# Attention row maxima: the third maximum of a step as two 256-key matmuls, and the second score pair's exponentials one bank each

## Chip, cores and metric

The kernel runs on one NeuronCore of a Trainium2 chip. The metric is the device time of one execution in microseconds (us). Before the change it is 3601.7 us, the median of 3 runs (3599.2 to 3603.54).

## What is computed

Two layers of two sublayers each on x of shape 2048 x 512, in float32. The first sublayer mixes by a Fourier transform, written as matmuls with given matrices. The second is attention with 32 heads of width 16 that share one key and one value head:

```python
q = (x @ wq).reshape(B, S, H, Dh).transpose(0, 2, 1, 3)
k = x @ wk
v = x @ wv
scores = jnp.einsum("bhqd,bkd->bhqk", q, k) * (Dh ** -0.5)
p = softmax(scores, axis=-1)
o = jnp.einsum("bhqk,bkd->bhqd", p, v)
return o.transpose(0, 2, 1, 3).reshape(B, S, H * Dh) @ wo
```

Each sublayer is added to its input, which is layer-normalised first.

## The kernel before

Each layer has a phase A (Fourier mixing, layer norm, queries, keys, values) and a phase B (attention). The change lies in phase B and in the short preparation at the end of phase A. The order of the instructions is written out by hand in the code; nothing reorders them. The tile pools add the waits: a write into a tile waits until the tile's earlier readers are done, and a read until its writers are.

**Steps.** Phase B has 16 query tiles of 128 rows (`i`), and 32 steps for each (`s_`): two halves of the heads by 16 chunks of 128 keys. A step (`phase_b`, the loop at L1049) does four things.

- Four *scores* (`score`, L879): matmuls of 64 contraction rows by 512 columns (four pairs of heads by 128 queries). `j` is 0 to 3; `j % 2` is the half of the array's rows (0 to 63 or 64 to 127) that a matmul uses, since even and odd heads lie on different halves. Two matmuls on different halves can run side by side. Scores 0 and 1 go to the two banks of one PSUM tile `x`, scores 2 and 3 to those of another (`pair`, two buffers of two banks). When both scores of a pair are issued, one exponential of 1024 elements reads both banks (ScalarE, L899).
- Up to three *maxima* for a later query tile (`max_half`, L435, by way of `more_max`): a matmul of 64 rows by 512 keys for one head into a bank `y` (three buffers), then a maximum over its 512 elements on VectorE into the tile `mxp` (`reduce_max`, recorded at L102). The row maximum is subtracted inside the score matmul, through extra contraction rows, so the maxima of a tile must be ready before its scores start. `units` lists all (tile, pair, half, key block) in order, `owed` keeps three per step.
- The *value matmuls* (`pv`, L903) of the step two before: four matmuls of 128 rows by 512 into four column groups of one bank `z`. Each is two records in the trace.
- At given steps, pieces of the output projection of the tile before (`out_tasks`), stores and loads, and `max_neg`, `max_split` and `max_rows`, which turn `mxp` into the extra rows.

In TensorE's queue a step is: value matmuls, first score, one maximum, second score, two maxima, third score, fourth score. With `g` the half of the next maximum, the scores are issued so that matmuls on different halves alternate: `1-g`, max `g`, `g`, max `1-g`, max `g`, `1-g`, `g`.

In the last tile of a layer, once all maxima are done, scores 2 and 3 go to banks `y` of their own, with an exponential of 512 elements each (L889 and L891).

`mxp` holds for each pair and half the maxima of 4 key blocks (5 for tile 0). `max_neg` takes the maximum over them.

Of the kernel before, what the change touches and what calls it, by code (L numbers as in the profile page):

```python
# [17 lines left out]
P = 128  # L18
# [3 lines left out]
DH = 16  # L22
# [25 lines left out]
def fnet_mqa_kernel(ctx: ExitStack, tc: tile.TileContext, x_in, ct, dt_, wq, wkv, wo, out):  # L48
# [5 lines left out]

    def f(ap):
        return ap.bitcast(F32)

    class Pace:
        pe = dve = act = pool = at = 0.0
# [61 lines left out]
    def pair():  # L121
        return ps.tile([P, 2, 512], F32, name="x", bufs=2)
# [127 lines left out]
    def make_layer(L, src, mid, dst, last):  # L250
# [138 lines left out]

        def partial(i):  # L390
            if i not in o.mxp:
                o.mxp[i] = sb.tile([P, NPAIR, 2, 4 if i else 5], F32, name=f"mxp{i % 4}")
                for e, (i_, kb) in enumerate(KEPT):
                    if i == i_:
                        np_ = taken[i, kb]
                        if np_:
                            pool.tensor_copy(o.mxp[i][:, :np_, :, kb], st["mxe"][:, e, :np_])
            return o.mxp[i]
# [36 lines left out]
        def max_half(i, pr, g, kb):  # L435
            pm = bank("y")
            gs = slice(64 * g, 64 * g + KR)
            mm(pm, o.qT[i][gs, pr, :], kz[gs, kb * 512:kb * 512 + 512], start=True, stop=True)
            vec.reduce_max(partial(i)[:, pr, g, kb:kb + 1], pm, axis=AX.X)

        def qT_load(i, k=None):
            k_ = QSLOT[i] if k is None else k
            if k_ in ("h", "l"):
                qt = (xnh if k_ == "h" else xnl)[:, 12:, :].rearrange("p t n -> p (t n)")
            else:
                qt = slot(k_, F32R)
            nc.sync.dma_start(f(qt), qd[i])
            o.qT[i] = qt.rearrange("p (a q) -> p a q", a=NPAIR)
            if k is None:
                o.loaded.add(i)  # L450

        def max_neg(i, p0=0, n=NPAIR, k=4, whole=False):
            nm = sb.tile([P, NPAIR, 2], F32, name="nm")[:, :n, :]
            vec.tensor_reduce(nm, o.mxp[i][:, p0:p0 + n, :, :k], op=ALU.max, axis=AX.X, negate=True)
            if p0 + n == NPAIR:
                o.mxp.pop(i)
            st["nm"] = nm
            if whole:
                max_split()

        def max_split():
            nmv = st.pop("nm").rearrange("p a g -> p g a")
            n = nmv.shape[2]
            ms = sb.tile([P, 2, 2, NPAIR], F32, name="ms").rearrange("p g r a -> p (g r a)")
            ms = ms[:, :4 * n].rearrange("p (g r a) -> p g r a", g=2, r=2)
            vec.tensor_copy(ms[:, :, 0, :].bitcast(F32R), nmv)
            vec.tensor_sub(ms[:, :, 1, :].bitcast(F32R), nmv, ms[:, :, 0, :])
            st["ms"] = ms
# [170 lines left out]
        def phase_a(extra):  # L639
# [211 lines left out]
            for e, left in ahead.items():  # L851
                assert EARLY[e][0]
                taken[EARLY[e][:2]] = NPAIR - len(left)
            units.extend((0, pr, g, 3) for pr in range(HALF, NPAIR) for g in range(2))
            units.extend((i, pr, g, kb) for i in range(1, NT) for pr in range(NPAIR) for kb in range(4) for g in range(2)
                         if pr >= taken.get((i, kb), 0))
            max_neg(0, 0, HALF, 5, True)
            for k in range(12):
                more_max()
                if k == 2:  # L860
                    max_rows(0, 0, HALF, nc.scalar)

        units = []
        o.done = o.extra = 0

        def more_max():
            if o.done < len(units) and units[o.done][0] in o.loaded | {0}:
                max_half(*units[o.done])
                o.done += 1

        def owed(n):
            return min(3 * (n + 1) + 12 + o.extra, len(units)) - o.done

        def done_with(i, pr):
            return all(u[:2] > (i, pr) for u in units[o.done:])

        ptiles = {}

        def score(i, s_, j):  # L879
            hf, c = divmod(s_, NT)  # L880
            jj, g = divmod(j, 2)
            cp = 4 * (2 * hf + jj)
            if (i, s_) not in ptiles:
                k = i * NSTEP + s_
                ptiles[i, s_] = slot((6, 7, 2)[k % 3]).rearrange("p (j n) -> p j n", j=4)
            w = j // 2
            if i == NT - 1 and jj == 1 and o.done == len(units):
                e = bank("y")
                nc.tensor.matmul(e, kz[64 * g:64 * g + KR, c * P:(c + 1) * P],  # L889
                                 o.qT[i][64 * g:64 * g + KR, cp:cp + 4, :], start=True, stop=True)  # L890
                nc.scalar.activation(ptiles[i, s_][:, j, :], e, AF.Exp, scale=DH ** -0.5)  # L891
                return
            first = "e" not in st
            if first:
                st["e"] = pair()
            nc.tensor.matmul(st["e"][:, g, :], kz[64 * g:64 * g + KR, c * P:(c + 1) * P],  # L896
                             o.qT[i][64 * g:64 * g + KR, cp:cp + 4, :], start=True, stop=True)
            if not first:
                nc.scalar.activation(ptiles[i, s_][:, 2 * w:2 * w + 2, :], st.pop("e"), AF.Exp, scale=DH ** -0.5)  # L899

        acc = {}

# [62 lines left out]
        def o_proj(i):  # L965
            for k in range(NK):
                o_mm(k)
                if k == NK - 1:
                    o_add(i)
                if k % 2 and 3 <= i < NT - 1:  # L970
                    for _ in range(2):
                        more_max()
                        o.extra += 1

        def o_add(i):
            nc.vector.tensor_add(bt["x"], bt["po"], bt["x"])
# [61 lines left out]
        def phase_b(nxt):  # L1038
# [7 lines left out]
            for j in range(NK):  # L1046
                wo_load(j)
            behind = []
            for n in range(NT * NSTEP):  # L1049
                i, s_ = divmod(n, NSTEP)  # L1050
                if len(behind) == 2:
                    pv(*behind.pop(0))
                behind.append((i, s_))
                g = units[o.done][2] if o.done < len(units) else 1
                for j, m in ((1 - g, 1), (g, 2), (3 - g, 0), (2 + g, 1)):
                    score(i, s_, j)
                    for _ in range(m):
                        if owed(n) >= 1:
                            more_max()
                if i == 0 and 2 <= s_ <= 8 and s_ % 2 == 0:  # L1060
                    q_half_store(14, s_ // 2 - 1)
                if n == 12:
# [13 lines left out]
                for at, j, p0, np_ in ((NT - AHEAD, i, HALF, HALF), (NSTEP - AHEAD, i + 1, 0, HALF if i == NT - 2 else NPAIR)):  # L1076
                    if j in (0, NT - 1) or j == i + 1 < NT:
                        if s_ == at:
                            assert done_with(j, p0 + np_ - 1), (n, j, o.done, len(units), units[o.done], owed(n))
                            max_neg(j, p0, np_)  # L1080
                        if s_ == at + 1:
                            max_split()
                        if s_ == at + 2:
                            max_rows(j, p0, np_)
# [71 lines left out]
```

## Time and profile before

One execution was profiled. It took 3602.02 us as a whole, and its span in the profile is 3600.2 us.

| what | value |
|---|---|
| median of 3 runs | 3601.7 us |
| profiled execution: its time, its span | 3602.02 us, 3600.2 us |
| phase B of layer 0, from its first to its last value matmul | 644.2 to 1800.4 us |
| phase B of layer 1, the same | 2433.2 to 3588.2 us |
| granted TensorE clock over the span | 0.997 of full speed |

How to read the lines that the prediction shows: in a timeline row stand the start, the duration, the engine, the line of the code, the operation, the tile written and the tiles read, the shapes and how many were merged; in brackets the idle time of that engine before it and what ended it. PE is TensorE's matmuls, PEld its weight loads, DVE VectorE, ACT ScalarE, POOL GpSimd. Matmuls are pipelined, and the end of a matmul is modelled. In a table of stretches each engine has its busy time with the number of instructions; then follow the granted TensorE clock, the DMA share and GB/s.

### The profile page before, as it was taken

The numbers are of one execution on the slowest core, as the hardware profiler recorded it, in microseconds if no ns is written. First come the engines' busy times: TensorE is split into PE (matmuls) and PEld (weight loads), VectorE is DVE, ScalarE is ACT, GpSimd is POOL, SyncE is SP. The second block draws the span as 40 slices with busy tenths as digits, with TensorE's granted clock in tenths as the row PEclk, the third lists the DMA queues.
The fourth block names the chain that finished last, engine by engine and source line by source line (L and its number), as shares of the span: only waits on it lengthen the run. The fifth ranks groups of instructions, "written<-read, shape, count | busy, mean of one in ns | idle before, by whom it ended". The sixth has DMA issues, their size and how long they took to land.

```text
span 3600.2 us, 63751 instructions
## 1 busy us (share of the span) xinstructions
PE 3551.6 (99%) x25090; PEld 1901.3 (53%) x25090; DVE 2801.6 (78%) x4819; ACT 2390.8 (66%) x3050; POOL 781.9 (22%) x976
## 2 busy tenths in 40 slices
PE   8999999999999999999999999999999999999999
PEld 6787877434333433343377878773433343333433
DVE  6186987888888888888311979878888888888882
ACT  4323232888888888888933232229888888888888
POOL 5544342011211111111264343420000000000000
PEclk9999999999999999999999999999999999999999
DMA  5544242211111100110144343422111111011100
GB/s 181 140 140 134 99 137 60 75 49 37 34 32 51 34 23 22 49 34 25 40 141 113 128 118 106 130 60 86 34 35 34 50 35 34 22 29 43 35 24 25
DMA packets 204445, 240.85 MB, mean 67 GB/s; under 512 B 36848, under 2 KB 160752, under 8 KB 197232
## 3 DMA queue, kind: packets, MB, share of 16 engines
q1 hardware_dynamic: 199216, 219.98, 20.5%
q0 software_dynamic: 4864, 16.78, 1.6%
q8 instruction: 196, 3.21, 0.4%
q14 instruction: 105, 0.86, 0.1%
q10 hardware_dynamic: 64, 0.02, 0.0%
HBM read 172.48 MB, written 63.17 MB: 65 GB/s over the span
## 4 chain that ended last, share of the span: by engine, by line
PE 85%; DVE 7%; ACT 2%; issue 1%; DMA 1%; SPq 0%; POOL 0%; DVEq 0%; ACTq 0%; POOLq 0%
PE z L910 27%; PE y L78 19%; PE x L896 19%; PE x L78 17%; DVE mxp L102 4%; PE z L78 1%; DVE mxe L102 1%; ACT slot L899 1%; PE z L83 1%; ACT slot L891 0%; PE y L889 0%; DVE row L102 0%; DVE bst L102 0%; DVE ms L102 0%; PE y L83 0%
## 5 line engine op out<-in xcount | busy, mean ns | idle before, releaser
L102 DVE TENSOR_REDUCE mxp<-y 128x1 f32<-128x512 f32 (+1 forms) x3472 | 2166.7, 679 | 267.3 <-PE y L78 218.1
L899 ACT ACTIVATE slot<-x 128x1024 f32<-128x1024 f32 x1992 | 1943.4, 1027 | 313.6 <-PE x L896 226.4
L910 PE MATMUL z<-slot,v 128*32 128x512 f32 x8192 | 1096.4, 605 | 1.7 <-ACT row L913 1.7
L78 PE MATMUL y<-kz,slot 64*128 64x512 f32 (+1 forms) x3048 | 980.1, 424 | 4.4 <-DVE kz L102 2.1
L896 PE MATMUL x<-slot,kz 64*128 64x512 f32 x2960 | 891.2, 447 | 0.8 <-DMA slot<-mt 0.8
L896 PEld LDWEIGHTS x<-slot,kz 64*128 64x128 f32 x2960 | 368.1, 185 | 734.3 <-ACT slot L899 599.7
L78 PEld LDWEIGHTS y<-kz,slot 64*128 64x128 f32 x3048 | 487.8, 185 | 121.8 <-DVE mxp L102 26.5
L78 PE MATMUL x<-ch,xnh 64*128 64x512 f32 (+2 forms) x2048 | 531.6, 372 | 11.7 <-ACT xnh L102 9.5
L78 PE MATMUL x<-ch,xnl 64*128 64x512 f32 (+2 forms) x2048 | 527.8, 364 | 1.0 <-POOL xnl L102 0.6
L78 PE MATMUL x<-cl,xnh 64*128 64x512 f32 (+2 forms) x2048 | 524.3, 364 | 0.4 <-POOL cl L102 0.4
L950 POOL TENSOR_TENSOR row<-row,row 128x256 f32<-128x256 f32 x63 | 46.3, 734 | 1573.7 <-DMA row<-rd 1184.2
L102 POOL TENSOR_TENSOR cl<-craw,ch 128x512 fp32r<-128x512 f32 x244 | 318.0, 1321 | 298.2 <-ACT ch L102 243.0
L78 PEld LDWEIGHTS x<-ch,xnh 64*128 64x128 f32 (+1 forms) x2048 | 293.1, 185 | 63.4 <-issue 16.2
L78 PEld LDWEIGHTS x<-ch,xnl 64*128 64x128 f32 (+1 forms) x2048 | 298.7, 185 | 38.0 <-POOL xnl L102 4.4
L78 PEld LDWEIGHTS x<-cl,xnh 64*128 64x128 f32 (+1 forms) x2048 | 295.0, 185 | 32.2 <-POOL cl L102 0.7
L910 PEld LDWEIGHTS z<-slot,v 128*32 128x32 f32 x8192 | 163.7, 108 | 274.6 <-issue 247.5
L102 ACT COPY junk<-x 128x2 f32<-128x2 f32 x236 | 37.7, 160 | 350.6 <-PE x L78 328.0
L102 DVE TENSOR_REDUCE mxe<-y 128x1 f32<-128x512 f32 x408 | 257.1, 679 | 9.8 <-PE y L78 9.6
L102 ACT CAST ch<-craw 128x512 fp32r<-128x512 f32 x264 | 158.8, 620 | 155.7 <-PE x L78 120.2
L78 PE MATMUL y<-slot,slot 128*128 128x512 f32 x816 | 216.4, 406 | 8.2 <-DVE mxp L102 6.7
L78 PEld LDWEIGHTS y<-slot,slot 128*128 128x128 f32 x816 | 144.7, 188 | 63.1 <-issue 28.2
L896 PE MATMUL x<-xnl,kz 64*128 64x512 f32 x512 | 154.5, 443 | 0.3 <-DMA xnl<-mt 0.3
(126 smaller groups left out, 2576.9 us busy)
## 6 DMA issues: line engine op xcount, KB each, us to landing
craw<-ct_in SPq DMA_DIRECT2D x112, 512.0 KB
slot<-qd SPq DMA_DIRECT2D x42, 1024.0 KB
qd<-row SPq DMA_DIRECT2D x144, 128.0 KB
od<-row SPq DMA_DIRECT2D x252, 64.0 KB
row<-x_in SPq DMA_DIRECT2D x32, 256.0 KB
mid<-row POOLq DMA_DIRECT2D x32, 256.0 KB, 2.6
craw<-ct_in SPq DMA_DIRECT2D x32, 256.0 KB
row<-mid SPq DMA_DIRECT2D x32, 256.0 KB
```

What stands on the lines that cost most here:

```text
L78: nc.tensor.matmul(out_, w, x, **k)
L83: nc.tensor.transpose(out_, x, i_)
L102: return fn(out_, in_, *a, **k)
L896: nc.tensor.matmul(st["e"][:, g, :], kz[64 * g:64 * g + KR, c * P:(c + 1) * P], o.qT[i][64 * g:64 * g + KR, cp:cp + 4, :], start=True, sto ...
L899: nc.scalar.activation(ptiles[i, s_][:, 2 * w:2 * w + 2, :], st.pop("e"), AF.Exp, scale=DH ** -0.5)
L910: nc.tensor.matmul(a[32 * j:32 * j + 32, :], v1[:, c, :], pt[:, j, :], start=c == 0, stop=c == NT - 1)
L950: nc.gpsimd.tensor_mul(bt["ot"][:, cs], bt["ot"][:, cs], bt["den"][:, cs])
```

## The change

Per step, two of the maxima stay whole 512-key matmuls, one on each half of the rows, now issued together as a pair (`max_whole`). The third (`max_couple`) covers half of a key block, 256 keys, for both heads of a pair: one 256-key matmul on half 0 as the first of the step's 64-row matmuls, one on half 1 as the last, both into one bank, and one VectorE maximum over 2 x 256 elements. Two row halves write one bank, so an explicit dependency keeps them apart: `relay` puts a no-op on ScalarE that waits for the first 256-key matmul, and the second waits for the no-op. The second 256-key half of the block is taken up in the next step that owes a maximum, and gets a column of its own; so `mxp` has 6 columns, of which unused ones are filled by a GpSimd memset, and `max_neg` reads 6. `max_neg` and `max_split` use parts of the tiles `row0` or `row2` for their results.

The two `x` tiles of the scores are now allocated once per layer (`o.pairs`). Scores are issued in the order 1, 0, 3, 2. The first pair keeps its exponential of 1024 elements (`exp_pair`). In the second pair each score is followed by an exponential of 512 elements of its own.

```diff
+    def behind_(later, first):
+        tc.add_manual_dep(later.ins, first.ins.name,
+                          mybir.DependencyInfo(mybir.DependencyClass.Sync, mybir.DependencyReason.DATA), reason="row halves")
...
-                o.mxp[i] = sb.tile([P, NPAIR, 2, 4 if i else 5], F32, name=f"mxp{i % 4}")
+                o.mxp[i] = sb.tile([P, NPAIR, 2, 6], F32, name=f"mxp{i % 4}")
+                nc.gpsimd.memset(o.mxp[i][:, HALF if i == 0 else 0:, :, 4:6], -3.0e38)
...
+        def max_whole(i, pr, kb):
+            for g in range(2):
+                max_half(i, pr, g, kb)
+
+        def max_couple(i, pr, kb, h, g):
+            if g == 0:
+                st["couple"] = bank("y").rearrange("p (g c) -> p g c", g=2)
+            gs = slice(64 * g, 64 * g + KR)
+            c0 = 512 * kb + 256 * h
+            m = nc.tensor.matmul(st["couple"][:, g, :], o.qT[i][gs, pr, :], kz[gs, c0:c0 + 256], start=True, stop=True)
+            if g == 0:
+                st["first"] = m
+                return
+            behind_(m, st.pop("relay"))
+            k = kb
+            if h:
+                k = 4 + o.coupled.get((i, pr), 0)
+                o.coupled[i, pr] = k - 3
+                assert k < 6
+            nc.vector.reduce_max(partial(i)[:, pr, :, k], st.pop("couple"), axis=AX.X)
+
+        def relay():
+            st["relay"] = nc.scalar.nop()
+            behind_(st["relay"], st.pop("first"))
...
-        def max_neg(i, p0=0, n=NPAIR, k=4, whole=False):
-            nm = sb.tile([P, NPAIR, 2], F32, name="nm")[:, :n, :]
+        def max_neg(i, p0=0, n=NPAIR, k=6, whole=False):
+            st["gather"] = half(0 if i or p0 else 2)
+            nm = st["gather"][:, 64:64 + 2 * n].rearrange("p (a g) -> p a g", g=2)
...
-            first = "e" not in st
-            if first:
-                st["e"] = pair()
-            nc.tensor.matmul(st["e"][:, g, :], kz[64 * g:64 * g + KR, c * P:(c + 1) * P],
+            e = o.pairs[w]
+            nc.tensor.matmul(e[:, g, :], kz[64 * g:64 * g + KR, c * P:(c + 1) * P],
                              o.qT[i][64 * g:64 * g + KR, cp:cp + 4, :], start=True, stop=True)
-            if not first:
-                nc.scalar.activation(ptiles[i, s_][:, 2 * w:2 * w + 2, :], st.pop("e"), AF.Exp, scale=DH ** -0.5)
+            if w:
+                nc.scalar.activation(ptiles[i, s_][:, j, :], e[:, g, :], AF.Exp, scale=DH ** -0.5)
+
+        def exp_pair(i, s_):
+            nc.scalar.activation(ptiles[i, s_][:, :2, :], o.pairs[0], AF.Exp, scale=DH ** -0.5)
...
+            o.pairs = [pair(), pair()]
             for n in range(NT * NSTEP):
                 i, s_ = divmod(n, NSTEP)
                 if len(behind) == 2:
                     pv(*behind.pop(0))
                 behind.append((i, s_))
-                g = units[o.done][2] if o.done < len(units) else 1
-                for j, m in ((1 - g, 1), (g, 2), (3 - g, 0), (2 + g, 1)):
-                    score(i, s_, j)
-                    for _ in range(m):
-                        if owed(n) >= 1:
-                            more_max()
+                whole = pick_whole(n)
+                couple = pick_couple(n)
+                if couple:
+                    max_couple(*couple, 0)
+                score(i, s_, 1)
+                score(i, s_, 0)
+                if couple:
+                    relay()
+                exp_pair(i, s_)
+                if whole:
+                    max_whole(*whole)
+                score(i, s_, 3)
+                score(i, s_, 2)
+                if couple:
+                    max_couple(*couple, 1)
```

TensorE's queue over one step in the middle of phase B of layer 0, before the change. `x` are the scores, `y` the maximum's matmuls, `z` the value matmuls; a bracket names the engine whose semaphore the matmul waits for:

```order
L896 MATMUL x<-xnl,kz 128x512 [waits Activation_49]
L78 MATMUL y<-kz,slot_9473 128x512 [waits DVE_49]
L896 MATMUL x<-xnl,kz 128x512
L78 MATMUL y<-kz,slot_9473 128x512 [waits DVE_49] x2
L896 MATMUL x<-xnl,kz 128x512 [waits Activation_49]
L896 MATMUL x<-xnl,kz 128x512
L910 MATMUL z<-slot_11376,v_74 32x512 x4
```

The first score of each pair waits for ScalarE (Activation), the second does not. The same place after the change:

```order
L455 MATMUL y<-kz,slot_10386 128x256 [waits DVE_49]
L945 MATMUL x<-xnl,kz 128x512 x2
L82 MATMUL y<-kz,slot_10386 128x512 [waits DVE_49] x2
L945 MATMUL x<-xnl,kz 128x512 [waits Activation_49] x2
L455 MATMUL y<-kz,slot_10386 128x256 [waits Activation_sequencer_49]
L962 MATMUL z<-slot_11630,v_74 32x512 x4
```

The 256-key matmuls stand first and last; the scores of the first pair (1 and 0) carry no wait of their own, and both scores of the second pair (3 and 2) wait for ScalarE. ScalarE's queue over one step after the change:

```order
L951 ACTIVATE slot_12958<-x 128x1024 [waits PE_49,Activation_49]
L948 ACTIVATE slot_12958<-x 128x512 [waits PE_49] x2
```

Before, two exponentials of 1024 elements stood there. Now one of 1024 is followed by two of 512, score 3's and then score 2's, each waiting for its own matmul (PE); the no-op of `relay` stands ahead of them and is not shown.

## Prediction before the run

> **What bounds the kernel now.** I read the page first (busy shares, slices, chain), then the time of the two attention phases, then one step of them instruction by instruction. Four lines of the page:
>
> ```profile
> span 3600.2 us, 63751 instructions
> ...
> PE 3551.6 (99%) x25090; PEld 1901.3 (53%) x25090; DVE 2801.6 (78%) x4819; ACT 2390.8 (66%) x3050; POOL 781.9 (22%) x976
> ...
> PEclk9999999999999999999999999999999999999999
> ...
> PE 85%; DVE 7%; ACT 2%; issue 1%; DMA 1%; SPq 0%; POOL 0%; DVEq 0%; ACTq 0%; POOLq 0%
> ```
>
> TensorE is busy throughout and carries 85% of the chain that ended last. The change touches only the loop over 512 steps in each attention phase. Those phases are the stretches below (busy time of TensorE, its weight loads, VectorE, ScalarE, GpSimd, then the granted clock):
>
> ```profile
> 644.20:1800.40 1156.20, 1149.78 (x7811) 455.38 (x7809) 975.63 (x1698) 1001.48 (x1083) 168.10 (x346) 1.00 0.13 38
> 2433.20:3588.20 1155.00, 1148.23 (x7814) 454.72 (x7812) 964.05 (x1608) 1001.65 (x1083) 64.55 (x106) 1.00 0.13 37
> ```
>
> One step in order of time. PEld is a weight load; L896 are score matmuls, L78 y the maximum's matmuls, L910 the value matmuls, L899 the exponentials, L102 the maxima on VectorE:
>
> ```profile
> 1201.62 1.94 ACT L899 ACTIVATE slot<-x 128x1024 f32<-128x1024 f32 x2 [0.18 <-PE y L78]
> ...
> 1202.93 0.18 PEld L896 LDWEIGHTS x<-slot,kz 64*128 64x128 f32 x1 [0.84 <-ACT slot L899]
> 1202.93 0.49 PE L896 MATMUL x<-slot,kz 64*128 64x512 f32 x1
> ...
> 1202.93 0.49 PE L78 MATMUL y<-kz,slot 64*128 64x512 f32 x1
> ...
> 1203.26 0.39 PE L896 MATMUL x<-slot,kz 64*128 64x512 f32 x1
> 1203.26 0.63 PE L78 MATMUL y<-kz,slot 64*128 64x512 f32 x2
> ...
> 1203.49 1.89 DVE L102 TENSOR_REDUCE mxp<-y 128x1 f32<-128x512 f32 x3
> 1203.62 0.18 PEld L896 LDWEIGHTS x<-slot,kz 64*128 64x128 f32 x2
> 1203.62 0.50 PE L896 MATMUL x<-slot,kz 64*128 64x512 f32 x2
> 1203.75 1.94 ACT L899 ACTIVATE slot<-x 128x1024 f32<-128x1024 f32 x2 [0.18 <-PE y L78]
> ...
> 1204.05 0.16 PEld L910 LDWEIGHTS z<-slot,v 128*32 128x32 f32 x8 [0.24 <-issue]
> 1204.05 1.06 PE L910 MATMUL z<-slot,v 128*32 128x512 f32 x8
> ...
> 1205.04 0.18 PEld L896 LDWEIGHTS x<-slot,kz 64*128 64x128 f32 x1 [0.84 <-ACT slot L899]
> ```
>
> A step is 1205.04 - 1202.93 = 2.11 us (I use 2.12, the next one's length). ScalarE works 1.94 and VectorE 1.89 of it. The chain that ended last shows how TensorE fills the step:
>
> ```profile
> 1203.00 0.42 PE x L896
> 1203.42 0.00 PE y L78
> 1203.42 0.23 PE x L896
> 1203.65 0.24 PE y L78 x2
> 1203.89 0.23 PE x L896 x2
> 1204.12 0.99 PE z L910 x8
> ```
>
> Seven 64-row matmuls run in four places: two pairs, then one busy only on one half of the rows, then a pair (0.42 with the change of array shape, 0.23, 0.24, 0.23), then 0.99 of value matmuls. So TensorE bounds the step, and the third maximum costs a place of its own (0.24). ScalarE's slack is 0.18 us, VectorE's 0.23.
>
> **The change part by part.** *The split maximum.* Two 256-key matmuls replace one of 512: columns per half of the rows go from 2048 and 1536 to 1792 and 1792. If the halves pack perfectly, half a place goes: 0.12 us of 2.12. If matmuls start strictly as issued, the order (256 on half 0, score 1, score 0, whole maximum on half 0, whole maximum on half 1, ...) leaves half 1 waiting behind half 0 and gives nothing. Gain per step: 0 to 0.12.
>
> *ScalarE's relay* waits for the first 256-key matmul, ahead of an exponential that waits for a matmul issued later. It is hidden there: 0. The same holds for VectorE, which still has three 512-element maxima per step; for max_neg, which reads 6 columns rather than 4; and for one GpSimd memset per tile, GpSimd being busy 22% of the span.
>
> *The exponentials one bank each.* Here the order of waits changes, and this term decides. In the rows of TensorE in the section on the change, both matmuls of the second score pair now wait for ScalarE; before, only the first of the two did. The first (score 3) waits for the last exponential of the step before. Whatever ScalarE did earlier is done by then, so a second wait on ScalarE, by score 2 right behind it, can only be for something later. ScalarE's only later work on that pair of banks ahead of score 2 is the exponential of score 3 *of the same step*. The program treats the two banks as one tile: a write into one waits for the read of the other. So score 2 cannot start before the first pair's exponential and then score 3's have ended, and the value matmuls, queued behind score 2, wait too. The chain of one step, from the weight load of its first matmul:
>
> - To the start of the first pair's exponential: now 1203.75 - 1202.93 = 0.82. The second score follows a 512-column matmul on its half there and a 256-column one afterwards, 0.11 sooner: 0.71 (from 0.59, if it follows nothing, to 0.82).
> - To the start of score 3's exponential, and its duration. The last tile has 512-element exponentials (minimum, median and maximum in ns), here behind a 1024-element one:
>
> ```profile
> L891 ACT ACTIVATE slot<-y x112: 591/748/768, 1746.1 to 3589.3; 128x512 f32<-128x512 f32 x112
> ```
>
> ```profile
> 3553.33 1.02 ACT L899 ACTIVATE slot<-x 128x1024 f32<-128x1024 f32 x1 [2.76 <-PE x L896]
> 3554.25 1.08 ACT L891 ACTIVATE slot<-y 128x512 f32<-128x512 f32 x2
> ```
>
>   3554.25 - 3553.33 = 0.92 to its start; then 0.59, the minimum. The median of 0.75 belongs to stretches where ScalarE has no gap at all; after the change it has gaps. I take 0.59 and keep 0.75 for the range.
> - From the end of that exponential to score 2's weight load: the exponentials begun at 1201.62 end at 1203.56, the waiting load starts at 1203.62: 0.06.
> - From that load to the first value load: 1204.05 - 1203.62 = 0.43. The second 256-key matmul lies beside score 2.
> - Value matmuls to the next step's first load: 1205.04 - 1204.05 = 0.99.
>
> Sum: 0.71 + 0.92 + 0.59 + 0.06 + 0.43 + 0.99 = 3.70 us for 2.12, or +1.58. Any packing gain (0.12) is already in the 0.71; packing further on is cover under ScalarE's 0.92. Other waits fit in: score 2's own exponential (0.59) ends beside the 0.99 of value matmuls, and VectorE's 1.89 fits into 3.70, so no bank of the maxima is missed.
>
> How many steps: the page's row of the exponentials is
>
> ```profile
> L899 ACT ACTIVATE slot<-x 128x1024 f32<-128x1024 f32 x1992 | 1943.4, 1027 | 313.6 <-PE x L896 226.4
> ```
>
> With 112 exponentials in line 891, two to a step, 56 of the 1024 steps take the other branch (one bank each already, in separate tiles) and stay. 968 x 2 + 56 = 1992 agrees. So 968 x 1.58 = 1529 us come on top. What some steps carry besides (output projection, transposes, stores) comes behind score 2 and costs what it does now. The profiled execution took 3602.0 us (span 3600.2), 0.3 above the median of 3601.7: 3602 + 1529 = **5131 us**, and I say 5130.
>
> **Rivals.** *The clock gate (chance 0.12).* TensorE will do less in each step. Score 3 ends some 1.0 to 1.1 us into it (0.42 + 0.23 + 0.24 + 0.23 less 0.12, and the end of a matmul's record), and score 2 loads at 0.71 + 0.92 + 0.59 + 0.06 = 2.28: a wait of 1.2 to 1.3 us in 3.70. Before the change the granted clock fell in thin places. Stretches of 3.41 us, each with TensorE's busy time and matmul count, then the clock as the seventh figure:
>
> ```profile
> 2405.24:2408.66 3.42, 2.64 (x18) 2.00 (x18) 2.83 (x5) 1.21 (x4) 1.47 (x2) 1.00 0.47 96
> 2408.66:2412.07 3.41, 2.38 (x18) 2.14 (x18) 0.69 (x1) 0.94 (x2) 0.00 (x0) 1.00 0.50 102
> ...
> 2422.31:2425.72 3.41, 2.33 (x8) 0.86 (x6) 3.13 (x6) 0.68 (x2) 0.73 (x1) 1.00 0.00 0
> 2425.72:2429.14 3.42, 3.32 (x8) 1.88 (x8) 3.42 (x7) 1.28 (x1) 0.00 (x0) 0.50 0.34 77
> ```
>
> Busy 2.64 and 2.38 with 18 matmuls kept the clock; busy 2.33 with 8 matmuls lost it for the next stretch. A step of the changed kernel has 16 matmul records (four scores, two whole and two half maxima, eight of values), and a stretch of 3.41 us with the whole wait in it is busy for 3.41 - 1.2 = 2.2: thin enough in time, not in count. At half clock the 0.43, the 0.99 and of the 0.71 about 0.45 (its shape change and two matmuls, 0.42 + 0.23 less what overlaps) double: +1.87, a step of 5.57, and 3602 + 968 x 3.45 = 6940 if all steps are hit; a third of them gives about 5730.
>
> The Trainium skill, TensorE: Matmul & The Clock Gate, "What's actually happening", says that the clock drops after an idle window of about 3.4 us. By that rule nothing happens here, as the wait is well under 3.4, and the sum stays at 5131. The trace does not agree in full: 2.33 of 3.41 us were busy where the clock was lost. The same page, "A second HAM failure mode", says that short idles between groups of matmuls can suffice, and by that rule the 6940 would hold.
>
> *Score 2 does not wait for score 3's exponential (0.03).* This is the case on the other side: each bank waits for its own last read alone. Then the step is TensorE's again, 2.12 less 0.12 at best. ScalarE's 0.92 + 2 x 0.48 (1.08 - 0.59 = 0.49 in the rows above) = 1.9 and VectorE's 1.89 fit into 2.00, and the time is 3602 - 968 x 0.12 = 3486; with matmuls strictly as issued it is 3602. It decides from the moment that score 2's wait is met before score 3's exponential ends. Against it stands the second wait in the rows, which has nothing earlier left to wait for.
>
> The Trainium skill, PSUM — Partial Sum Buffer, "PSUM bank collisions raise a hardware error", has two engines run clean on different banks, so the chip itself would not need this wait; no run here shows that. What executes is the wait that the program carries.
>
> **How the numbers follow.** Forecast 0.85, clock gate 0.12, no wait 0.03. The likeliest gives 5130. Its own bounds are a step of 3.70 - 0.12 (nothing ahead of the second score) and 3.70 + 0.11 (as now) + 0.16 (exponential of 0.75): 3602 + 968 x 1.46 = 5015 to 3602 + 968 x 1.85 = 5393. I give 5000 to 5390, which leaves out the two rivals and a rest of the forecast, less than 2 in 10 together. About 0.2% is what a measurement of this kernel tells from no change. Slower 0.97 (forecast and clock gate); of the last rival's 0.03, faster 0.02 and same 0.01.
>
> **What would show it.** Right: in one step, a gap on TensorE of 1.2 to 1.4 us between score 3 and score 2, with the weight load of a score waiting for the 512-element exponential in about 968 steps, over 1,200 us in total; steps of 3.7 us; VectorE's busy total unchanged near 2,800 us, now 55% of the span; ScalarE's up by about 150 (two of 0.59 for one of 1.03), near 50%; the chain handing over between TensorE and ScalarE in every step. Clock gate: PEclk below 9 in slices of the attention phases, and steps near 5.6. Wrong: both scores of the second pair side by side and steps of 2.0 to 2.2 us.

## The result, and the profile after

| | before | after |
|---|---|---|
| median (lowest to highest, runs) | 3600.55 us (3599.2 to 3603.54, 4) | 5143.69 us (5131.74 to 5155.91, 4) |
| ratio, 95% interval | 1 | 1.4284, 1.4249 to 1.432 |
| profiled execution: time, span | 3602.02 us, 3600.2 us | 5144.49 us, 5142.7 us |
| granted clock over the span | 0.997 | 0.982 |

The change costs 1,543 us, 43%. Forecast were 5130 us and a range of 5000 to 5390.

From the page of the changed kernel: the span, the busy times, the granted clock in 40 slices, and the chain that ended last, by engine and by line.

```profile
span 5142.7 us, 67751 instructions
...
PE 3851.5 (75%) x26058; PEld 1982.4 (39%) x26058; DVE 2900.5 (56%) x4819; ACT 2566.3 (50%) x4018; POOL 782.4 (15%) x1008
...
PEclk9999999999899999999999999999999999999999
...
PE 61%; ACT 30%; issue 3%; DVE 3%; ACTq 0%; POOL 0%; DMA 0%; DVEq 0%; SPq 0%; POOLq 0%
PE z L962 21%; ACT slot L951 20%; PE x L82 12%; PE x L945 12%; ACT slot L948 9%; PE y L82 7%; PE y L455 6%; DVE mxp L106 1%; PE z L82 1%; DVE mxe L106 1%; PE z L87 0%; ACT slot L942 0%; ACTq L951 0%; DVE row L106 0%; PE y L940 0%
```

TensorE was busy 99% of the span and carried 85% of the chain. Now it is busy 75% and carries 61%, and ScalarE 30%: the exponential of the first pair (L951, 20%) and those of the second (L948, 9%). No engine is full.

The view of the waits of the changed kernel (engine, tile, line and what it waited for: us in total, times, longest):

```profile
PEld x L945 <- ACT slot L948: 1686.1, 968, 2.1
PE x L945 <- ACT slot L948: 1253.4, 968, 1.6
```

In 968 steps the weight load of a score waits for a 512-element exponential; the matmuls stand idle 1,253 us for it, 1.29 us each time. One step of the changed kernel in order of time:

```profile
1216.84 0.18 PEld L455 LDWEIGHTS y<-kz,slot 64*128 64x128 f32 x1 [0.84 <-DVE mxp L465]
1216.84 0.38 PE L455 MATMUL y<-kz,slot 64*128 64x256 f32 x1
...
1216.84 0.61 PE L945 MATMUL x<-xnl,kz 64*128 64x512 f32 x2
...
1217.18 0.51 PE L82 MATMUL y<-kz,slot 64*128 64x512 f32 x2
...
1217.41 0.39 PE L945 MATMUL x<-xnl,kz 64*128 64x512 f32 x1
1217.55 1.02 ACT L951 ACTIVATE slot<-x 128x1024 f32<-128x1024 f32 x1 [1.00 <-PE x L945]
...
1218.47 0.59 ACT L948 ACTIVATE slot<-x 128x512 f32<-128x512 f32 x1
...
1219.11 0.18 PEld L945 LDWEIGHTS x<-xnl,kz 64*128 64x128 f32 x1 [1.75 <-ACT slot L948]
1219.11 0.50 PE L945 MATMUL x<-xnl,kz 64*128 64x512 f32 x1 [1.31 <-ACT slot L948]
...
1219.54 0.16 PEld L962 LDWEIGHTS z<-slot,v 128*32 128x32 f32 x8 [0.24 <-issue]
...
1219.65 0.60 ACT L948 ACTIVATE slot<-x 128x512 f32<-128x512 f32 x1 [0.59 <-PE x L945]
...
1220.54 0.18 PEld L455 LDWEIGHTS y<-kz,slot 64*128 64x128 f32 x1 [0.84 <-DVE mxp L465]
```

The reader can follow the chain by starts. First load 1216.84; first pair's exponential 0.71 later; score 3's exponential 0.92 after that, for 0.59; score 2's load 0.05 behind its end, 1.31 us after TensorE's last matmul; value matmuls 0.43 later; the next step's first load 1.00 after these. Together 1220.54 - 1216.84 = 3.70 us.

### The profile page after: what moved, and what is told of

It reads as the page before. It is cut to its first block, busy times and chain, and to the rows that moved or that the text cites. A ratio compares the mean times of both kernels' runs of the same rounds, so it can differ in the third digit from the quotient of the medians.

```text
span 5142.7 us, 67751 instructions
## 1 busy us (share of the span) xinstructions
PE 3851.5 (75%) x26058; PEld 1982.4 (39%) x26058; DVE 2900.5 (56%) x4819; ACT 2566.3 (50%) x4018; POOL 782.4 (15%) x1008
## 4 chain that ended last, share of the span: by engine, by line
PE 61%; ACT 30%; issue 3%; DVE 3%; ACTq 0%; POOL 0%; DMA 0%; DVEq 0%; SPq 0%; POOLq 0%
PE z L962 21%; ACT slot L951 20%; PE x L82 12%; PE x L945 12%; ACT slot L948 9%; PE y L82 7%; PE y L455 6%; DVE mxp L106 1%; PE z L82 1%; DVE mxe L106 1%; PE z L87 0%; ACT slot L942 0%; ACTq L951 0%; DVE row L106 0%; PE y L940 0%
## 5 line engine op out<-in xcount | busy, mean ns | idle before, releaser
L106 DVE TENSOR_REDUCE mxp<-y 128x1 f32<-128x512 f32 (+1 forms) x2504 | 1588.3, 677 | 1049.7 <-PE y L82 1047.3
L945 PE MATMUL x<-slot,kz 64*128 64x512 f32 x2960 | 1090.3, 455 | 921.1 <-ACT slot L948 921.1
L951 ACT ACTIVATE slot<-x 128x1024 f32<-128x1024 f32 x1024 | 1053.7, 1029 | 1071.5 <-PE x L945 1066.8
L948 ACT ACTIVATE slot<-x 128x512 f32<-128x512 f32 x1936 | 1151.0, 595 | 576.2 <-PE x L945 576.2
L465 DVE TENSOR_REDUCE mxp<-y 128x2 f32<-128x512 f32 x968 | 670.8, 693 | 659.0 <-PE x L945 659.0
L945 PEld LDWEIGHTS x<-slot,kz 64*128 64x128 f32 x2960 | 490.3, 188 | 1287.0 <-ACT slot L948 1239.8
L82 PE MATMUL y<-kz,slot 64*128 64x512 f32 (+1 forms) x2352 | 667.8, 407 | 5.1 <-DVE kz L106 2.1
L82 PE MATMUL x<-ch,xnh 64*128 64x512 f32 (+2 forms) x2048 | 530.4, 372 | 12.5 <-ACT xnh L106 10.4
L455 PE MATMUL y<-kz,slot 64*128 64x256 f32 x1392 | 539.5, 388 | 0.0
L82 PE MATMUL x<-ch,xnl 64*128 64x512 f32 (+2 forms) x2048 | 526.5, 364 | 0.9 <-POOL xnl L106 0.5
L82 PE MATMUL x<-cl,xnh 64*128 64x512 f32 (+2 forms) x2048 | 523.6, 364 | 0.4 <-POOL cl L106 0.4
L455 PEld LDWEIGHTS y<-kz,slot 64*128 64x128 f32 x1392 | 258.7, 186 | 598.5 <-DVE mxp L465 446.4
L82 PEld LDWEIGHTS y<-kz,slot 64*128 64x128 f32 x2352 | 373.4, 189 | 67.1 <-DVE mxp L106 25.4
L82 PEld LDWEIGHTS x<-ch,xnh 64*128 64x128 f32 (+1 forms) x2048 | 298.1, 185 | 62.3 <-issue 16.2
L82 PEld LDWEIGHTS x<-ch,xnl 64*128 64x128 f32 (+1 forms) x2048 | 303.6, 185 | 35.5 <-POOL xnl L106 4.2
L945 PE MATMUL x<-xnh,kz 64*128 64x512 f32 x512 | 189.8, 452 | 166.9 <-ACT slot L948 166.9
L82 PEld LDWEIGHTS x<-cl,xnh 64*128 64x128 f32 (+1 forms) x2048 | 299.8, 186 | 30.0 <-POOL cl L106 0.7
```

Source lines behind the costliest of these rows:

```text
L82: nc.tensor.matmul(out_, w, x, **k)
L106: return fn(out_, in_, *a, **k)
L455: m = nc.tensor.matmul(st["couple"][:, g, :], o.qT[i][gs, pr, :], kz[gs, c0:c0 + 256], start=True, stop=True)
L465: nc.vector.reduce_max(partial(i)[:, pr, :, k], st.pop("couple"), axis=AX.X)
L945: nc.tensor.matmul(e[:, g, :], kz[64 * g:64 * g + KR, c * P:(c + 1) * P], o.qT[i][64 * g:64 * g + KR, cp:cp + 4, :], start=True, stop=True)
L948: nc.scalar.activation(ptiles[i, s_][:, j, :], e[:, g, :], AF.Exp, scale=DH ** -0.5)
```

## The experiments

The theory: score 2 waits for score 3's exponential because the two banks are one tile, and this wait is all of the loss. The rivals: the clock gate; the split maximum with its bank or its relay; the greater number of exponentials. Kernels run together share runs of the kernel before, whose median was 3602.45, 3602.64, 3602.38 and 3600.91 us in the four groups. Diffs are against the changed kernel unless said otherwise.

### Take the wait away: three ways

**Order alone.** Both scores of the second pair are issued before their two exponentials.

```diff
             if w:
-                nc.scalar.activation(ptiles[i, s_][:, j, :], e[:, g, :], AF.Exp, scale=DH ** -0.5)
+                later.append((ptiles[i, s_][:, j, :], e[:, g, :]))
...
                 score(i, s_, 3)
                 score(i, s_, 2)
+                exp_later()
                 if couple:
```

> Both scores of the second pair are issued ahead of their two exponentials of 512; all else as changed. Theory (score 2 waits for score 3's exponential): that wait is gone, the step falls from 3.70 to 2.00 to 2.17 us and the time to 3490 to 3650. Rival ScalarE (the two short exponentials and their handovers are the cost in themselves): three exponentials one behind the other without overlap, 1.03 + 0.59 + 0.59 us and about 0.2 for each handover, 2.6 to 2.8 us a step, 4070 to 4260. Rival relay (the no-op's synchronisation of the 256-key matmuls is the cost): unchanged, 5140.

Measured: 3764.91 us (3763.32 to 3766.13), ratio to before 1.0451 (1.0436 to 1.0467), granted clock 0.997.

**Tiles alone.** The order of the change stays, but the second pair's banks are two tiles of one bank each.

```diff
...
-            e = o.pairs[w]
-            nc.tensor.matmul(e[:, g, :], kz[64 * g:64 * g + KR, c * P:(c + 1) * P],
+            e = o.pairs[w][g] if w else o.pairs[0][:, g, :]
+            nc.tensor.matmul(e, kz[64 * g:64 * g + KR, c * P:(c + 1) * P],
...
-            o.pairs = [pair(), pair()]
+            o.pairs = [pair(), [single(0), single(1)]]
...
```

> The second pair's two banks become two PSUM tiles of one bank each; the order of all instructions stays as changed (score 3, its exponential, score 2, its exponential). Theory: score 2 then waits for its own bank's exponential of the step before alone, and the time is 3490 to 3650, as with the scores first. Rival ScalarE: 4070 to 4260. Rival relay: 5140.

Measured: 3764.11 us (3762.48 to 3765.3), ratio 1.0449 (1.0434 to 1.0465).

**One exponential.** Only the split maximum and its relay of the change remain; the second pair gets one exponential of 1024 elements again.

```diff
-            if w:
-                nc.scalar.activation(ptiles[i, s_][:, j, :], e[:, g, :], AF.Exp, scale=DH ** -0.5)
...
                 score(i, s_, 2)
+                if not (i == NT - 1 and o.done == o.total):
+                    exp_pair(i, s_, 1)
```

> The other part of the change alone: split maximum and relay stay, the second pair has one exponential of 1024 behind both scores. Theory: 3490 (row halves pack, 0.12 us a step) to 3602 (matmuls start strictly as issued, so half 1 waits behind half 0 and nothing is gained); a gain of nothing is the likelier. Rival relay: 5140. Rival ScalarE: as the theory.

Measured: 3766.32 us (3765.14 to 3767.2), ratio 1.0456 (1.0439 to 1.0474).

What follows: each way takes some 1,378 us off, to within 3 us of the others. The second of them changes neither the order nor the number of exponentials, so the loss is the wait between the two banks of one tile, and two exponentials instead of one cost nothing beside it. But all three stop 162 to 164 us above the kernel before, and so above what was expected of them (at most 3650, for the third 3602): the split maximum by itself makes this kernel slower, which the prediction did not have.

### Put the wait alone into the kernel before, and double it

The kernel before, with the second pair's exponential cut into one per bank and nothing else:

```diff
+            if w:
+                nc.scalar.activation(ptiles[i, s_][:, j, :], st["e"][:, g, :], AF.Exp, scale=DH ** -0.5)
             if not first:
-                nc.scalar.activation(ptiles[i, s_][:, 2 * w:2 * w + 2, :], st.pop("e"), AF.Exp, scale=DH ** -0.5)
+                e = st.pop("e")
+                if not w:
+                    nc.scalar.activation(ptiles[i, s_][:, :2, :], e, AF.Exp, scale=DH ** -0.5)
```

> The kernel before with one part of the change alone: in the second score pair each score is followed by its own exponential of 512, both banks in one tile; the maxima stay three of 512 keys. Theory: the wait comes back without the split maximum. Step 0.82 + 0.92 + 0.59 + 0.06 + 0.43 + 0.99 = 3.81 us, 3602 + 968 x 1.69 = 5240. Rival relay: 3600 to 3650, since no relay is there. Rival ScalarE: 4070 to 4260.

Measured: 5786.12 us (one run). The waits view and the granted clock of its page:

```profile
PE x L896 <- ACT slot L899: 1276.4, 968, 1.7
```

```profile
PEclk9999877877777777777899997778877877778778
```

The same 968 waits. Where the clock held, the median step is 3.81 us, as worked out, against 3.70 with the half-place packing. But the granted clock was 0.827 over the span, so the time lies above the 5240 that was expected: here the clock gate, a rival for the changed kernel, came true in part. Steps wholly at half clock took 5.47 (median of 68), and the more frequent ones that were only partly at half clock 5.16 (median of 459).

The changed kernel, with the first pair's exponential cut as well:

```diff
-            if w:
-                nc.scalar.activation(ptiles[i, s_][:, j, :], e[:, g, :], AF.Exp, scale=DH ** -0.5)
+            nc.scalar.activation(ptiles[i, s_][:, j, :], e[:, g, :], AF.Exp, scale=DH ** -0.5)
...
-                exp_pair(i, s_)
```

> The changed kernel, with the first pair's exponential one bank each as well, in one tile: the suspected wait is doubled. Wait theory: a step becomes a chain of all four exponentials in which each pair's second score waits for the first one's exponential: 0.57 + 0.59 + 0.06 + 0.57 + 0.48 + 0.59 + 0.06 + 0.43 + 0.99 = 4.34 us where the clock holds, so 3602 + 968 x 2.22 = 5750 as a whole, and up to 6900 where the waits also cost the clock, as they did in the kernel before with split exponentials. Rival, only ScalarE's added time counts (one more exponential of 0.59 for half of 1.03 in each step, 0.15 us): about 5300.

Measured: 7458.8 us (one run), above the 6900. TensorE in its timeline, a step at full clock and, after the dots, one at half:

```profile
2500.86 0.38 PE L455 MATMUL y<-kz,slot 64*128 64x256 f32 x1
2500.86 0.49 PE L945 MATMUL x<-xnl,kz 64*128 64x512 f32 x1
2502.10 0.49 PE L945 MATMUL x<-xnl,kz 64*128 64x512 f32 x1 [0.75 <-ACT slot L947]
...
2503.77 0.49 PE L945 MATMUL x<-xnl,kz 64*128 64x512 f32 x1 [0.93 <-ACT slot L947]
...
2505.18 0.38 PE L455 MATMUL y<-kz,slot 64*128 64x256 f32 x1
...
2510.16 0.58 PE L455 MATMUL y<-kz,slot 64*128 64x256 f32 x1
...
2516.26 0.58 PE L455 MATMUL y<-kz,slot 64*128 64x256 f32 x1
```

Two waits now, of 0.75 and 0.93. The step at full clock is 2505.18 - 2500.86 = 4.32 for the 4.34 worked out, so the chain of waits is right. The steps at half clock take 6.10, and most are of that kind: the granted clock over the span was 0.611.

### What holds the split maximum back

In the kernel with tiles of their own, long and short steps alternate in many places. One of them:

```profile
1206.01 1.29 DVE L106 TENSOR_REDUCE mxp<-y 128x1 f32<-128x512 f32 x2 [0.67 <-PE y L82]
...
1207.17 0.18 PEld L467 LDWEIGHTS y<-kz,xnl 64*128 64x128 f32 x1 [0.84 <-DVE mxp L106]
...
1207.21 0.69 DVE L477 TENSOR_REDUCE mxp<-y 128x2 f32<-128x512 f32 x1
...
1207.95 0.18 PEld L82 LDWEIGHTS y<-kz,xnl 64*128 64x128 f32 x1 [0.37 <-DVE mxp L477]
...
1209.73 0.18 PEld L467 LDWEIGHTS y<-kz,xnl 64*128 64x128 f32 x1 [0.84 <-DVE mxp L106]
...
1211.76 0.18 PEld L467 LDWEIGHTS y<-kz,xnl 64*128 64x128 f32 x1 [0.84 <-DVE mxp L106]
```

One step takes 1209.73 - 1207.17 = 2.56, the next 1211.76 - 1209.73 = 2.03. In the long one the second whole maximum (L82) waits for the read of the split maximum of the step before (L477); the view of the waits has this 428 times. That bank is taken by the first matmul of a step and read last, after the two whole maxima, in the next step. There are three banks `y`, so the second whole maximum needs just this one, and scores 3 and 2 queue behind it. The 2.03 shows that the packing does give its 0.1 us where nothing waits. The relay, the other suspect, does not appear among the waits of this kernel: no matmul and no weight load waits for the no-op.

**The values earlier.** The value matmuls go between scores 3 and 2, so that they lie beside score 3's exponential.

```diff
-                if len(behind) == 2:
-                    pv(*behind.pop(0))
-                behind.append((i, s_))
...
                 score(i, s_, 3)
+                if len(behind) == 2:
+                    pv(*behind.pop(0))
+                behind.append((i, s_))
                 score(i, s_, 2)
```

> As changed, but the value matmuls of a step stand between score 3 and score 2. Score 2 waits as before for score 3's exponential; the 0.99 us of value matmuls now lie beside that wait instead of behind it. Theory: first pair's scores to the start of its exponential 0.60 (no change of array shape ahead of them), 0.92, 0.59, 0.06, then score 2 in 0.34 and the next step right behind it: 2.51 us a step, 3602 + 968 x 0.39 = 3980, and no loss of clock. Rival ScalarE (time of the exponentials themselves): no change against the changed kernel, 5140. Rival banks (the wait matters little, the third maximum's bank held over the step sets the time): 5140 or more.

Measured: 4413.17 us (one run), with this row among its waits:

```profile
PEld y L82 <- DVE mxp L465: 591.2, 896, 0.7
```

The exponential does end beside the value matmuls, and the clock held (0.995). But a step is 2.97 us and not the 2.51 expected. The chain that ended last goes round in it from VectorE's read of the split maximum (0.70) to the whole maxima that wait for it (0.50), score 3 (0.24), the value matmuls (0.99), score 2 and the second 256-key matmul (0.47), and to the next read. So the bank of the split maximum holds the step, which the expectation did not count.

**The other half first.** With one exponential per pair, the whole maximum on half 1 is issued ahead of that on half 0 (the diff is against that kernel).

```diff
         def max_whole(i, pr, kb):
-            for g in range(2):
+            for g in (1, 0):
```

> As the kernel with the split maximum and one exponential (3766), but of the two whole maxima the one on half 1 is issued first. Theory banks (the split maximum's bank is taken by the step's first matmul and read last on VectorE, so the next step's second whole maximum waits for it): no help, 3700 to 3770. Rival order (half 1 waits behind half 0, as matmuls start as issued): 0.12 us a step are packed, 3490 to 3655.

Measured: 3658.76 us (3655.99 to 3660.42), ratio to before 1.0156 (1.0139 to 1.0173): some 108 us less than without the swap, on the mean 0.11 us in each of 968 steps. Neither range holds it: it lies 41 us below the 3700 of the banks and 4 us above the 3655 of the order, so both play a part. The trace agrees with matmuls that start in the order of issue. Unswapped, the first whole maximum needs half 0, where score 0 still runs, and starts 0.45 us (median) behind the step's first matmul; swapped, it starts beside score 0, 0.34 behind it, and VectorE's reads of the whole maxima start sooner too. The wait for the bank is still there:

```profile
PEld y L82 <- DVE mxp L465: 183.1, 689, 0.4
```

**The swap with tiles of their own.** The kernel with tiles of their own, and the same swap.

> The changed kernel, with the second score pair's banks as two separate tiles and the two whole maxima issued with half 1 first. Held-bank theory (the bank of the split maximum, taken by the first matmul of the step and read last on VectorE, sets the step once the wait between the scores is gone; the swap gives 0.11 us a step as it did with one exponential of 1024): 3640 to 3670. Rival, the exponential of 1024 elements had still held the second pair back, so that the release of each bank by itself brings more now: 3540 to 3600, below the kernel before.

Measured: 3655.41 us (3653.19 to 3656.13), ratio 1.0147 (1.013 to 1.0164). It lies in the range of the held-bank theory: the way in which the exponentials are cut hardly matters here. Still slower than before by some 53 us.

**The split maximum across two steps.** In the kernel with one exponential and the swap, the first 256-key matmul stands last in a step, and the second one in the next step, first (first run below) or third (second run). This was to hold the bank for a shorter time on TensorE. The diff is of the first run; in the second, `couple_second()` stands behind score 0.

```diff
                 couple = pick_couple(n)
-                if couple:
-                    max_couple(*couple, 0)
+                couple_second()
                 score(i, s_, 1)
...
                 if couple:
-                    max_couple(*couple, 1)
+                    couple_first(*couple)
```

> As the swapped kernel, but the two 256-key matmuls that share a bank are the last of one step (half 1) and the first of the next (half 0), so the bank is held over the value matmuls instead of over a step's scores, and VectorE reads it first in the next step. Theory banks: the wait for the bank goes. What is left is a loop over two steps: end of the second exponential to its scores' weights 0.06, on to the values 0.43 to 0.54, values 0.99, to the next first exponential 0.71, 0.92, 1.02: 4.13 to 4.24 for two steps, 2.07 to 2.12 a step, 3550 to 3610. Rival (the split maximum costs in itself, by VectorE's two-row read or by the relay): 3700 to 3770.

> As the last one, but the 256-key matmul on half 0 stands third, behind scores 1 and 0, so nothing is ahead of the first pair. Theory banks and loop: to the first exponential 0.60 instead of 0.71, two steps in 4.02 to 4.13, 2.01 to 2.07 a step, 3500 to 3555, faster than before. Rival (the split maximum costs in itself): 3700 to 3770. Rival relay: the no-op stands behind the second pair's exponential on ScalarE and the third matmul waits for it, 0.1 to 0.3 us a step more: 3600 to 3850.

Measured: 3987.19 us (3986.16 to 3988.14), ratio 1.1067 (1.1051 to 1.1084), with the second matmul first; 4201.32 us (4199.85 to 4202.9), ratio 1.1662 (1.1645 to 1.1679), with it third. Both lie far above every range that was given. One step of the former, in which L462 is the second 256-key matmul, L953 the exponentials, L469 the read of the split maximum and L453 the first 256-key matmul of the next one:

```profile
1300.87 1.94 ACT L953 ACTIVATE slot<-x 128x1024 f32<-128x1024 f32 x2 [0.54 <-PE x L949]
...
1301.64 0.16 PEld L964 LDWEIGHTS z<-slot,v 128*32 128x32 f32 x8
...
1302.64 0.18 PEld L462 LDWEIGHTS y<-kz,slot 64*128 64x128 f32 x1 [0.84 <-ACTq L472]
...
1303.06 0.69 DVE L469 TENSOR_REDUCE mxp<-y 128x2 f32<-128x512 f32 x1 [0.59 <-PE y L462]
...
1303.81 0.18 PEld L453 LDWEIGHTS y<-kz,slot 64*128 64x128 f32 x1 [0.53 <-DVE mxp L469]
...
1305.12 0.18 PEld L462 LDWEIGHTS y<-kz,slot 64*128 64x128 f32 x1 [0.84 <-ACTq L472]
```

From the waits, first of the former and then of the latter run:

```profile
PEld y L453 <- DVE mxp L469: 503.6, 960, 0.6
PE y L453 <- DVE mxp L469: 308.9, 959, 0.4
```

The weight load of L462 is put down to the relay's no-op (L472), but the relay does not hold the step. The 0.84 us in the bracket is time in which only the weight loads stand idle, beside the value matmuls, as it was in the kernel before. L462 starts 1.00 us behind the first value matmul, just as the step's first matmul does in the changed kernel, and at 1302.64, ahead of the end of the exponentials at 1302.81; in 849 of 968 steps an exponential still runs when it starts. The loss comes behind it: L453 starts 0.06 us behind the end of VectorE's read, in 960 steps, and the value matmuls queue behind L453. So it is the bank again. The next split maximum is begun in the same step now, and it takes the bank that was read last. A step is 1305.12 - 1302.64 = 2.48 us, and in the second run 2.71 (median), where TensorE itself stands idle 0.32 us for this read in 959 steps.

**Free the bank sooner.** The kernel with tiles of their own and the swap, in which VectorE's last read is made shorter (the diff is against that kernel).

```diff
-            nc.vector.reduce_max(partial(i)[:, pr, :, k], st.pop("couple"), axis=AX.X)
+            nc.vector.reduce_max(partial(i)[:, pr, :, k], st.pop("couple")[:, :, :64], axis=AX.X)
...
```

> The changed kernel with the second pair's banks as two separate tiles and half 1's whole maximum first, and with VectorE's read of the split maximum cut to 64 of the 256 columns of each half (the matmuls stay whole). It leaves out the other columns of that maximum, and its exponentials work with a sixteenth of the scale so that they stay finite; what they compute is not the softmax of the reference. Held-bank theory: the read ends some 0.4 us earlier, the bank of the split maximum is free before the next step's second whole maximum wants it, and the wait of 182 us in 689 steps goes: 3655 - 182 = 3473, or 3486 if the packing of the half place (0.12 us a step) is the limit; I expect 3460 to 3510, below the kernel before. Rival, TensorE's order of starts holds the step and the wait for the bank only fills time that is lost anyway: 3635 to 3660.

Measured: 3593.14 us (3590.02 to 3594.55), ratio 0.9976 (0.9966 to 0.9986). It falls by 62 us, not by the 145 or more that were expected, and not by the rival's 0 to 20. Its timeline shows both why it falls and what is late next:

```profile
1203.56 0.18 PEld L467 LDWEIGHTS y<-kz,slot 64*128 64x128 f32 x1 [0.84 <-DVE mxp L106]
...
1205.19 1.08 ACT L961 ACTIVATE slot<-xs 128x512 f32<-128x512 f32 x2
...
1205.58 0.18 PEld L467 LDWEIGHTS y<-kz,slot 64*128 64x128 f32 x1 [0.84 <-DVE mxp L106]
...
1206.32 0.18 PEld L958 LDWEIGHTS xs<-slot,kz 64*128 64x128 f32 x1 [0.21 <-ACT slot L961]
...
1207.75 0.18 PEld L467 LDWEIGHTS y<-kz,slot 64*128 64x128 f32 x1 [0.84 <-DVE mxp L106]
```

A step of 2.02 and one of 2.17. No whole maximum waits for the bank any more, and the first of the two steps has the packed length. In the other, score 2 waits for the last exponential of the step before, begun at 1205.19 with its pair and ended at 1206.27. So with the bank out of the way ScalarE is the next to hold a step, by 0.92 + 1.08 us of exponentials. The view of the waits has that wait 484 times, every second step. This is read from the trace; no run shortens ScalarE's work.

**Control.** The kernel before with half-length reads of its maxima (the diff is against the kernel before).

```diff
-            vec.reduce_max(partial(i)[:, pr, g, kb:kb + 1], pm, axis=AX.X)
+            vec.reduce_max(partial(i)[:, pr, g, kb:kb + 1], pm[:, :256], axis=AX.X)
...
```

> Control: the kernel before, with VectorE's read of every maximum of the three per step cut to 256 of 512 columns (matmuls whole) and the same sixteenth of the scale in its exponentials; it leaves out the other columns of the maxima. If VectorE's time and its banks cost nothing in the kernel before (its matmuls wait 34 us in all for the reads of these banks), the time stays at 3595 to 3605. Rival, shorter reads help any order of this loop: below 3570.

Measured: 3578.96 us (3577.51 to 3580.44), ratio 0.9937 (0.9922 to 0.9952). Not the 3595 to 3605, and not below 3570. Set step against step, the some 750 steps without extra work keep their 2.12 us; 20 of the 22 us lie in the steps with an output projection or other extra work. In the kernel with the shorter split read it is the other way round: the 62 us lie in the steps without extra work. So the bank costs what it costs because of the split, not in any order of this loop.

No version that does the whole computation beats the kernel before. A fourth bank `y` was not tried: the two pairs, three `y` and `z` take all eight.

## Why the prediction was right, point by point

- *The chain of one step* was forecast as 0.71 + 0.92 + 0.59 + 0.06 + 0.43 + 0.99 = 3.70, and measured as 0.71, 0.92, 0.59, 0.05, 0.43 and 1.00, 3.70. That the wait is the cause is shown by its removal in three ways and by its addition to the kernel before.
- *How the wait was found* is weaker than the prediction has it. It argued that score 2's own wait for ScalarE can only be for something later, as score 3 already waits for the last exponential of the step before. That holds only if both banks wait as one tile, which was to be shown. With a wait for each bank, score 3 waits for its own bank's exponential and score 2 for the last one of the step before, as it does in the kernel with the shorter split read; so a second wait does not tell the two apart. What tells them apart are the idle 1.31 us that end with score 3's exponential, and the kernel with tiles of their own. The chance of 0.03 for the other case was too low for such an argument.
- *968 steps* changed, and 1,253 us of idle matmuls stand in the waits, as forecast (over 1,200).
- *The sum* gave 5131, measured were 5144.5 in the profiled execution. That it is low by only 13 us is in part luck, as what it left out nearly cancels. Set step against step, 40 steps that ran wholly or partly at half clock grew by 1.58 each and some 46 us on top; steps with extra work grew by less than 1.58 (one by 1.35, from 6.38 to 7.73), some 30 us in all; and the plain steps fell short of 1.58 by some 4 us in all. 46 - 30 - 4 = 12 of the 13 us.
- *The half-clock step* of the rival was put at 5.57 and is 5.26 (below): its matmuls did not double throughout, 0.71 became 1.11 and not 1.16, 0.43 became 0.72, 0.99 became 1.87.
- *VectorE* was to stay near 2,800 us and has 2900.5. Three maxima a step ran into one another before (1.89); now the split one stands alone for 0.69 beside 1.29 for two, 0.09 more in each of 968 steps. It lies inside the 3.70 and costs nothing. *ScalarE* got 175 us more, not 150: in a step it works 1.51 for the first two exponentials, which overlap, and 0.60 for the third, 2.11 for the 1.94 before.
- *The rival without a wait* was put at 3486 to 3602; it is 3764. Here the working failed. It let the split maximum gain between 0 and 0.12 us a step, because VectorE's 1.89 of work fits into 2.00. Work fits, but the bank's turn does not: it is held from the first matmul of a step into the next step. Beside the wait of 1.31 us this had cover, and the forecast said so for the changed kernel only ("no bank of the maxima is missed"), which held.

## What to carry over

When one instruction that reads two banks is cut in two, look at what unit the waits go by: if both banks are one tile, the second writer waits for the first reader of the same round, and the cut turns parallel work into a chain. Count for every buffer how long a round holds it, from its first writer to the end of its last reader in that engine's order, and not only how much work each engine has. Hold an idle time of the weight loads against the starts of the matmuls before it is called a cost: the 0.84 us beside the value matmuls cost nothing, whatever ends them. And price a change without its worst part as well: here what remained was itself slower by 4.5%, and the next two limits, a bank and then ScalarE, each showed up only when the one above was gone.

## What the runs showed of the hardware

*The clock falls without an idle stretch.* Stretches of 3.41 us of the changed kernel, each with the busy time of TensorE, its weight loads, VectorE, ScalarE and GpSimd with their counts, then the granted clock, the DMA share and GB/s:

```profile
1357.96:1361.37 3.41, 2.09 (x16) 0.73 (x16) 1.98 (x3) 2.11 (x3) 0.00 (x0) 1.00 0.00 0
1361.37:1364.78 3.41, 2.09 (x20) 0.87 (x16) 1.71 (x3) 1.97 (x3) 0.00 (x0) 1.00 0.02 5
...
1368.20:1371.61 3.41, 2.09 (x17) 0.73 (x9) 2.11 (x5) 1.92 (x3) 0.00 (x0) 1.00 0.00 0
1371.61:1375.02 3.41, 3.41 (x16) 1.18 (x15) 0.95 (x3) 1.03 (x2) 0.00 (x0) 0.57 0.02 5
1375.02:1378.44 3.42, 2.40 (x11) 0.49 (x10) 1.91 (x3) 1.68 (x3) 0.00 (x0) 0.50 0.02 5
```

TensorE in the timeline of the same place, a step at half clock:

```profile
1373.48 0.58 PE L455 MATMUL y<-kz,xnh 64*128 64x256 f32 x1
...
1376.15 0.79 PE L945 MATMUL x<-slot,kz 64*128 64x512 f32 x1 [1.02 <-ACT slot L948]
...
1376.87 1.93 PE L962 MATMUL z<-slot,v 128*32 128x512 f32 x8
1378.74 0.58 PE L455 MATMUL y<-kz,xnh 64*128 64x256 f32 x1
```

Busy 2.09 of 3.41 with 16 to 20 matmuls kept the clock, and then busy 2.09 with 17 lost it: neither of the two figures that the prediction compared tells them apart. The wait in each step was 1.31. The Trainium skill, TensorE: Matmul & The Clock Gate, "What's actually happening", has the clock drop after an idle window of about 3.4 us; these rows do not agree, no stretch here is idle. Its section "A second HAM failure mode", on short idles between groups of matmuls, does agree. How much is lost differs widely between kernels that are much alike: 0.982 with one wait of 1.31 in 3.70 us, 0.827 with one wait of about 1.3 in 3.81, 0.611 with waits of 0.75 and 0.93 in 4.32, and 0.997 in every kernel whose waits were gone. What sets the point stays open.
